# Retention attention and a gated layer on one core: 128-token units in the first block, another order of W_in slabs, other engines for their casts

## The chip, the cores and the metric

The kernel runs on one core of a Trainium2 chip. A core has TensorE (PE) for matrix products, VectorE (DVE), ScalarE (ACT), GpSimd (POOL) and SyncE (SP), which here only issues transfers. PE reads its operands from the on-chip memory SBUF and writes into PSUM, eight banks of 2 KB per partition. Every engine works through its own written list of instructions in order; semaphores hold it where it needs what another engine or a transfer makes. The metric is the device time of one execution in microseconds (us).

## What is computed

```python
def _attn_ref(q, k, v):                      # batch 8, heads 8, 576 positions, 64 wide
    scores = scale * np.matmul(q, k.transpose(0, 1, 3, 2))
    gamma = 1.0 - 2.0 ** (-5.0 - np.arange(H))
    Dmat = np.where(rel >= 0, gamma[:, None, None] ** rel[None, :, :], 0.0)
    return np.matmul(scores * Dmat[None], v)

x = attn_out.transpose(0, 2, 1, 3).reshape(4608, 512)
h = x @ w_in                                 # 512 x 2048
g = h * np.cos(h)
return g @ w_out                             # 2048 x 512
```

Inputs and output are float32; the kernel works in bf16 on PE.

## The kernel before, in words

**Attention.** The decay is folded into V and Q, so a causal product of plain masks is left: each batch row is cut into chunks of 64 positions, and a running state (K transposed times V) carries the past. The chunks are worked in 37 *sessions*; the first eight are "big" ones, handled in pairs (0/1, 2/3, 4/5, 6/7). For a pair, SP loads K, Q and V (`load_kv` L433, `load_q` L452, 512 KB each). K is cast to bf16 (`cast_k`, L494 on DVE or POOL, L491 on ACT), Q and V are cast and scaled (`cast_q` L532, `cast_v` L515). PE transposes K and Q (`step_tk` L552, `step_tq` L565), and a copy brings the result to SBUF (`turn`, L541 on DVE, L540 on ACT). Then come the scores (`big_s`: PE L704, DVE mask L712, four masks a pair), the state (L738), its copy to `sbd` (`ev_st`, DVE L667), the products with V (L763) and with the state (L730), and the eviction into `xt`, the layer's input (`move`, ACT L680). Later sessions take smaller steps (L608, L617, L627, L638, mask L653), and their loads are smaller (L441, V cast L522). Late sessions do not use PE for the transposes but a DMA transpose issued by SP (`move_k` L574, `move_q` L580): `BYPE` in `schedule` is the first session for which this holds.

**The layer.** Tokens are worked in nine blocks of 512. `mlp1` is one *unit* of the first layer, one PSUM bank: four matmuls (depth 512) for each 128 columns of W_in, either one such group over 512 tokens or several over fewer (PE L844); ACT makes the cosine (L852), DVE multiplies (L855) into `gt`. Block 0's second layer is a plain product (`mlp2`, L869). Blocks 1 to 8 use seven half-size products in place of eight (`strassen`, `product`, L963), for which DVE and POOL first make sums of `gt` (`token_sums`: L923, L928, L932) and DVE sums of W_out (`weight_sums`: L902, L908); the results are put together at L998, L1002 and L1007.

**Weights.** W_in comes in eight slabs of 256 columns (`load_win` L466, 512 KB each, f32), which land in tensors that are needed only later (`gt`, `s5`, `tw`: `staged`), and are cast into `win` (`cast_win`, L494 or L491). Slab s serves column groups 2s and 2s+1. W_out comes by four casting transfers from POOL (`load_wout` L483), held until a K load has landed.

**What sets the order.** `schedule` adds operations in a chosen sequence, `Prog.arrange` then plays them through a list scheduler with costs, a window for each engine and PSUM banks (`Box`), and writes the final order of every engine; until a planned time (`FILL`) it puts filler matmuls (`fill`, L828) where PE has nothing else. Constants steer it:

- `WP[s]`: the item of the load list ahead of which slab s is loaded. `WC[s]`: the engine that casts slab s.
- `EQ`, `C1`: engines for the casts of Q (two halves), for the first quads and for those after.
- `UNITS`: first-layer units of block 0 as (first token, last token, column groups). A unit takes 512 / (number of tokens) groups. `EARLY`: how many of them are added ahead of the attention of the next sessions.
- `G1`, `G2`: how many sessions' loads are listed at the start.
- `HOLD`: how many half products of `strassen` are kept back to the end of a block (the second number is for the last block but one).
- `POOLED`: from which block on the sum L928 runs on POOL instead of DVE.

The line of `schedule` that names the engines for the first four sessions is L1157, with the copy of K's transposes at L1159.

Of the kernel before, what the change touches and what calls it, by code (L numbers as in the profile page):

```python
# [18 lines left out]
TB = 512  # L19
NTB = TOK // TB  # L20
NB = 6
HOLD = (1, 4)
LS = (0, 1, 4, 2, 3, 5)
AT = (9, 11, 13, 15)
C1 = ('pool', ('pool', 'pool'), 'pool')
EO, ES, EQ = ('act', 'act'), ('dve', 'act'), ('dve', 'pool')
WP = (6, 5, 7, 8, 6, 9, 10, 9)
WC = ("pool", "act", "act", "pool", "pool", "act", "act", "dve")
G1, G2, WG = 3, 4, ("stg", 1, 1, 0)
EARLY = 2  # L30
SOFT = ()
SG = (1, 3)
UNITS = ((0, 256, (0, 10)), (256, 512, (0, 10)), (0, 512, (10, 16)))
FILL, SLOW = 24.0, 5.6
NF = DFF // 128
HF, HB = NF // 2, TB // 2
# [204 lines left out]


SOLO = 8
POOLED = 4
STB = 0


# [46 lines left out]
def new_in(g, of):  # L294
    was = {of(*x)[0] for y in SES[:g] for x in y}
    return [x for x in dict.fromkeys(of(*x)[0] for x in SES[g]) if x not in was]
# [6 lines left out]
class Kernel:  # L303
# [610 lines left out]
    def token_sums(self, j, u):  # L914
# [5 lines left out]
        def keys(k, *ts):  # L920
            return [("gt", j % 2, f + HF * k + i, x) for i in range(2) for t in ts for x in range(4 * t, 4 * t + 4)]
# [4 lines left out]
            r=keys(0, 0, 1) + keys(1, 0, 1), w=[("s5", f), ("s5", f + 1)], cost=0.62, port=True, lazy=True)  # L926
        eng = "pool" if j >= POOLED else "dve"
        self.P.add(eng, lambda e: e.tensor_tensor(  # L928
# [139 lines left out]
    def schedule(self):  # L1068
# [2 lines left out]

        need = [req(TB * (j + 1)) for j in range(NTB)]
        tiles, quads = ([new_in(g, of) for g in range(NS)] for of in (tile_of, quad_of))
        BYPE, LEAD = 14, 2
        at = {"load": 0, "cast": 0}

        def load_to(g, gate=()):
            while at["load"] < min(g, NS):
                x = at["load"]
                ts = [t for t in tiles[x] if t >= SOLO or t % 2 == 0]  # L1080
                for t in ts:
                    self.load_kv(t, 0, gate)
                for k in quads[x]:
                    self.load_q(k, gate)
                for t in ts:
                    self.load_kv(t, 1, gate)
                at["load"] += 1

        def cast_to(g, k="pool", q=("pool", "pool"), v="pool"):
            while at["cast"] < min(g, NS):  # L1090
                x = at["cast"]
                assert x < at["load"]
                for t in self.twos(tiles[x]):
                    self.cast_k(t, k)
                for y in quads[x]:
                    self.cast_q(y, q)
                for t in tiles[x]:
                    self.cast_v(t, v)
                at["cast"] += 1

        def T(g):
            if g >= NS:
                return
            if g < BYPE:
                for k in quads[g]:
                    self.step_tq(k, "dve")
                for t in self.twos(tiles[g]):
                    self.step_tk(t, "dve")
            x = g + LEAD
            if BYPE <= x < NS:  # L1110
                for k in quads[x]:
                    self.move_q(k)
                for t in tiles[x]:
                    self.move_k(t)
            cast_to(min(g + LEAD + 2, need[1]), *C1)
            cast_to(g + LEAD + 2)
            load_to(g + LEAD + 4)

        def run(mlp, att):
            n, m, k = len(att), len(mlp), 0  # L1120
            for i, u in enumerate(mlp):
                u()
                while k < n * (i + 1) // m:
                    att[k]()
                    k += 1

        def att_of(g0, g1):
            out = []
            for g in range(g0, g1):
                if BIG[g] or BIG[g - 1]:  # L1130
                    out.append(lambda g=g: self.step_s(g))
                out += [lambda g=g: T(g + 1), lambda g=g: self.step(g, not BIG[min(g + 1, NS - 1)]), lambda g=g: self.ev_st(g)]
            return out

        def m1(lo, hi, *fs):
            return lambda: self.mlp1(lo, hi, fs)
# [8 lines left out]
        def begin(lo, hi):  # L1145
            for i in range(lo, hi):
                for s in range(8):
                    if min(WP[s], len(items) - 1) == i and s not in SOFT and s - 1 not in SOFT:
                        self.load_win(s)
# [4 lines left out]
        for x, t in zip(SOFT, SG):  # L1154
            self.load_soft(x, [("stg", t, 0, 0)])
        for g in range(need[0]):
            cast_to(g + 1, "act", EQ, "dve" if g == 3 else "pool")  # L1157
            for t in self.twos(tiles[g]):
                self.step_tk(t, "dve")  # L1159
            for k in quads[g]:  # L1160
                self.step_tq(k, "dve")
            self.step_s(g)
            self.step(g, False, EO)
            self.ev_st(g, ES)
        begin(n0, len(items))
        for x in range(8):
            if x not in SOFT and x - 1 not in SOFT:
                self.cast_win(x, WC[x])
        for x in range(4):
            self.load_wout(x, [WG])  # L1170
        load_to(G2 + need[0], [("wout", 0)])
        cast_to(need[0] + 2, *C1)
        units = [(lo, hi, range(f, f + 512 // (hi - lo))) for lo, hi, fs in UNITS for f in range(*fs, 512 // (hi - lo))]
        for lo, hi, fs in units[:EARLY]:
            self.mlp1(lo, hi, fs)
        run([m1(lo, hi, *fs) for lo, hi, fs in units[EARLY:]], [lambda: T(need[0])] + att_of(need[0], need[0] + 2))
        sums = [x for y in zip(self.weight_sums(0), self.weight_sums(1)) for x in y]
# [6 lines left out]
        for j in range(1, NTB):  # L1184
# [3 lines left out]
            for f in range(0 if last else NF):  # L1188
                if j > 1:
                    mlp.append(m1(TB * (j + 1), TB * (j + 2), f))  # L1190
                elif f % 2 == 0:
                    mlp.append(m1(1280, 1536, f, f + 1))
                mlp += two[f:min(f + 1, 14 - HOLD[j + 2 == NTB])]
                if f in AT:
                    mlp.append(lambda u=AT.index(f), j=j: self.token_sums(j + 1, u))
            mlp += two[14 - HOLD[j + 2 == NTB]:14 if not last else 0]
            run(mlp, att_of(need[j + 1], need[j + 2]) if j + 2 < NTB else [])
# [38 lines left out]
```

## Time and profile before

| | us |
|---|---|
| median of 4 runs | 299.72 (299.58 to 300.63) |
| the profiled execution | 299.58 |
| its span | 297.8 |
| PE busy | 288.7 (97%) |
| DVE busy | 232.1 (78%) |
| ACT busy | 186.8 (63%) |
| POOL busy | 173.3 (58%) |

The granted TensorE clock is full (1.0). PE's busy time includes the filler, and the ends of pipelined matmuls are modelled, so a busy PE is not one at its peak. The averages hide stages: the first 20 us are set by loads, later ones by other things. In the rows of the profile, `bk` is a PSUM bank, `st` the state in PSUM, `stg` and `qstg` the f32 landing buffers of K, V and Q, `nat` and `qnat` their bf16 copies, `kt` and `qt` the transposed ones, `pt` the masked scores. A row gives its start, its length, engine, line, operation, output and input, the count, and in brackets the idle time ahead of it and what ended that.

### The profile page before, as it was taken

What the parts mean: (1) busy time and instruction counts of PE and PEld (TensorE: products, weight loads), DVE (VectorE), ACT (ScalarE), POOL (GpSimd) and SP (SyncE); (2) the same over time, 40 slices, a digit from 0 to 9 for tenths busy, and PEclk for the clock granted to TensorE, in tenths of its full rate; (3) what the DMA queues carried; (4) which work ended last, traced back from release to release, by engine and by line L of the source; (5) the groups of instructions that cost most, each with busy time, mean ns of one, the idle gap of its engine ahead of it and who ended that gap; (6) DMA issues with size and microseconds to landing.
All of it is one profiled execution on the core that took longest, in us unless ns stands there. A gap on an engine that the chain in (4) does not pass through costs nothing.

```text
span 297.8 us, 8942 instructions
## 1 busy us (share of the span) xinstructions
PE 288.7 (97%) x3751; PEld 203.7 (68%) x3751; DVE 232.1 (78%) x369; ACT 186.8 (63%) x317; POOL 173.3 (58%) x166
## 2 busy tenths in 40 slices
PE   6988899999999999999999999999999999999996
PEld 2557468765788885767566766676677577666685
DVE  6775899999789389679957995898489739964951
ACT  6256767836598286676667667766776777555521
POOL 4566650878847587287508992899274017402923
PEclk9999999999999999999999999999999999999999
DMA  7999999998999999989789988988201011102024
GB/s 207 303 327 325 279 192 218 207 220 207 201 247 209 192 277 203 220 170 200 166 183 234 203 175 212 212 149 191 59 33 60 16 44 40 45 19 70 2 70 143
DMA packets 123896, 50.13 MB, mean 168 GB/s; under 512 B 82384, under 2 KB 123344, under 8 KB 123856
## 3 DMA queue, kind: packets, MB, share of 16 engines
q1 hardware_dynamic: 121744, 47.46, 70.7%
q0 software_dynamic: 2112, 2.10, 4.3%
q8 instruction: 30, 0.49, 0.8%
q14 instruction: 10, 0.08, 0.1%
HBM read 36.70 MB, written 9.44 MB: 155 GB/s over the span
## 4 chain that ended last, share of the span: by engine, by line
PE 87%; SPq 4%; DMA 3%; DVE 3%; ACT 2%; issue 1%; DVEq 0%
PE bk L844 39%; PE bk L963 33%; PE bk L869 5%; DMA gt<-in_moe_w_in_dram 3%; PE st L638 2%; PE bk L617 2%; SPq L433 2%; SPq L466 1%; PE bk L608 1%; DVE gt L855 1%; PE bk L627 1%; PE bk L565 1%; SPq L452 1%; PE bk L552 1%; ACT xt L680 1%; DVE pt L712 1%
## 5 line engine op out<-in xcount | busy, mean ns | idle before, releaser
L844 PE MATMUL bk<-xt,win 128*128 128x512 bf16 (+1 forms) x744 | 138.9, 331 | 2.8 <-ACT win L491 0.7
L852 ACT ACTIVATE cb<-bk,cpi 128x512 bf16<-128x512 f32 x144 | 98.4, 688 | 55.2 <-PE bk L844 51.5
L855 DVE TENSOR_TENSOR gt<-bk,cb 128x512 bf16<-128x512 f32 x144 | 96.3, 684 | 41.8 <-ACT cb L852 36.5
L844 PEld LDWEIGHTS bk<-xt,win 128*128 128x128 bf16 x744 | 70.8, 98 | 43.7 <-issue 1.0
L532 POOL TENSOR_TENSOR qnat<-qstg,wt 128x512 bf16<-128x512 f32 x34 | 40.1, 1198 | 20.8 <-DMA qstg<-in_q_dram 19.0
L998 POOL TENSOR_TENSOR sv<-sv,os 128x512 f32<-128x512 f32 x16 | 20.4, 1273 | 49.1 <-ACT os L1007 36.3
L680 ACT ACTIVATE sbd<-st 64x512 bf16<-64x512 f32 x58 | 34.3, 592 | 11.7 <-PE bk L608 10.2
L494 POOL CAST nat<-stg 128x512 bf16<-128x512 f32 x32 | 24.7, 778 | 20.4 <-DMA stg<-in_k_dram 15.8
L928 POOL TENSOR_TENSOR s<-gt 128x512 bf16<-128x512 bf16 x20 | 28.8, 1448 | 13.4 <-DVE gt L855 13.4
L932 DVE TENSOR_TENSOR gt<-gt 128x1024 bf16<-128x1024 bf16 x32 | 34.1, 1067 | 0.2
L522 POOL TENSOR_TENSOR nat<-stg,wt 128x512 bf16<-128x512 f32 x28 | 32.1, 1147 | 2.4 <-DMA stg<-in_v_dram 1.9
L963 PE MATMUL bk<-tw,gt 128*128 128x256 bf16 x256 | 32.1, 273 | 0.0
L963 PE MATMUL bk<-wout,s 128*128 128x256 bf16 x256 | 31.6, 273 | 0.2 <-DVE s L923 0.2
L923 DVE TENSOR_TENSOR s<-gt 128x1024 bf16<-128x1024 bf16 x32 | 29.0, 916 | 3.1 <-PE bk L963 2.8
L963 PE MATMUL bk<-wout,gt 128*128 128x256 bf16 x256 | 30.8, 273 | 0.0
L680 ACT ACTIVATE xt<-bk 128x256 bf16<-128x256 f32 (+1 forms) x64 | 26.9, 488 | 4.2 <-DVE pt L653 3.6
L963 PEld LDWEIGHTS bk<-wout,s 128*128 128x128 bf16 x256 | 24.5, 98 | 6.5 <-DVE s L923 0.7
L963 PEld LDWEIGHTS bk<-tw,gt 128*128 128x128 bf16 x256 | 24.2, 98 | 6.0 <-ACT sv L1002 0.6
L963 PEld LDWEIGHTS bk<-wout,gt 128*128 128x128 bf16 x256 | 24.8, 98 | 4.4
L653 DVE TENSOR_TENSOR pt<-bk,tri 128x256 bf16<-128x256 f32 (+3 forms) x39 | 20.4, 543 | 0.8 <-PE bk L608 0.4
L1007 ACT ACTIVATE os<-bk 128x512 f32<-128x512 f32 x16 | 9.6, 597 | 12.0 <-PE bk L963 11.9
L998 POOL TENSOR_TENSOR sv<-sv 128x512 f32<-128x512 f32 x8 | 12.9, 1610 | 6.6 <-ACT sv L1002 6.3
(76 smaller groups left out, 276.6 us busy)
## 6 DMA issues: line engine op xcount, KB each, us to landing
out_dram<-os SPq DMA_DIRECT2D x31, 256.0 KB, 3.4
qstg<-in_q_dram SPq DMA_DIRECT2D x12, 512.0 KB, 5.8
stg<-in_k_dram SPq DMA_DIRECT2D x24, 256.0 KB, 4.5
stg<-in_v_dram SPq DMA_DIRECT2D x24, 256.0 KB, 5.1
stg<-in_k_dram SPq DMA_DIRECT2D x4, 512.0 KB, 7.6
stg<-in_v_dram SPq DMA_DIRECT2D x4, 512.0 KB, 7.4
gt<-in_moe_w_in_dram SPq DMA_DIRECT2D x4, 512.0 KB, 8.5
wout<-in_moe_w_out_dram POOLq DMA_DIRECT2D x4, 512.0 KB, 12.7
```

Of the source, the lines that this page charges most:

```text
L494: self.P.add(eng, lambda e: e.tensor_copy(dst, src), r=r, w=w, cost=cost, port=eng == "pool" or half == 0.75)
L522: self.P.add(eng, lambda e: e.tensor_tensor(ap(self.NAT[na], 2 * DM, 0, 128, DM, [D, H], [1, D]), ap(self.STG[st], 2 * DM, 0, 128, DM, [D, ...
L532: self.P.add(eng, lambda e, x=x: e.tensor_tensor(ap(self.QNAT[slot], 2 * DM, 0, 128, x * DM, [D, H], [1, D]), ap(self.QSTG[slot], 2 * DM, ...
L680: self.P.add(eng, (lambda e: e.activation(*io(), AF.Copy)) if eng == "act" else (lambda e: e.tensor_copy(*io())), r=r, w=w, cost=0.175 + 0 ...
L844: inst = e.matmul(self.bk(box.i, 0, 128, i * n, n), ap(self.WIN, 4 * DFF, 0, 128, c * DFF + 128 * f, [1, 128]), ap(self.XT, 4 * XR, 0, 128 ...
L852: self.P.add("act", lambda e: e.activation(ap(cb, TB, 0, 128, 0, [1, m]), self.bk(box.i, 0, 128, 0, m), AF.Sin, bias=self.CPI.ap(), scale= ...
L855: self.P.add("dve", lambda e: e.tensor_tensor(ap(gt, NF * TB, 0, 128, f0 * TB + lo - TB * j, [TB, len(fs)], [1, n]), self.half_bank(box.i, ...
L923: self.P.add("dve", lambda e: e.tensor_tensor(ap(self.S5, HF * TB, 0, 128, f * TB, [1, 2 * TB]), ap(gt, NF * TB, 0, 128, f * TB, [1, 2 * TB]),
L928: self.P.add(eng, lambda e: e.tensor_tensor(ap(self.S1, HF * HB, 0, 128, f * HB, [HB, 2], [1, HB]), half(0, 0), half(1, 1), ALU.add), r=ke ...
L932: self.P.add("dve", lambda e: e.tensor_tensor(ap(gt, NF * TB, 0, 128, f * TB + HB, [HF * TB - HB, 2], [TB, 2], [1, HB]), ap(gt, NF * TB, 0 ...
L963: inst = e.matmul(self.bk(box.i, 0, 128, at * HB, HB), ap(lt, lsize, 0, 128, loff + f * lstep + 128 * t, [1, 128]), ap(rt, rsize, 0, 128, ...
L998: self.P.add(eng, lambda e: e.tensor_tensor(out(), a(), b(), op), r=r, w=w, cost=1.2 if eng == "pool" else 0.09 + 0.00104 * n * HB, port=e ...
```

## The change

It sets other values for the constants, and other engines in two calls:

```diff
-HOLD = (1, 4)
+HOLD = (2, 4)
-C1 = ('pool', ('pool', 'pool'), 'pool')
-EO, ES, EQ = ('act', 'act'), ('dve', 'act'), ('dve', 'pool')
-WP = (6, 5, 7, 8, 6, 9, 10, 9)
-WC = ("pool", "act", "act", "pool", "pool", "act", "act", "dve")
-G1, G2, WG = 3, 4, ("stg", 1, 1, 0)
-EARLY = 2
+C1 = ('pool', ('dve', 'pool'), 'pool')
+EO, ES, EQ = ('act', 'act'), ('dve', 'act'), ('pool', 'dve')
+WP = (5, 6, 7, 6, 9, 8, 9, 7)
+WC = ("pool", "dve", "dve", "pool", "dve", "pool", "act", "act")
+G1, G2, WG = 5, 5, ("stg", 1, 1, 0)
+EARLY = 4
-UNITS = ((0, 256, (0, 10)), (256, 512, (0, 10)), (0, 512, (10, 16)))
+UNITS = ((0, 128, (0, 4)), (0, 256, (4, 8)), (128, 256, (0, 4)), (256, 512, (0, 8)), (0, 512, (8, 16)))
-POOLED = 4
+POOLED = 5
-        BYPE, LEAD = 14, 2
+        BYPE, LEAD = 15, 2
-            cast_to(g + 1, "act", EQ, "dve" if g == 3 else "pool")
+            cast_to(g + 1, "pool", EQ, "dve" if g < 2 else "pool")
             for t in self.twos(tiles[g]):
-                self.step_tk(t, "dve")
+                self.step_tk(t, "act")
```

- Block 0's first layer: the first 256 tokens of column groups 0 to 3 are worked as two units of 128 tokens by four groups; groups 4 to 7 keep 256-token units; groups 8 to 15 (before: 10 to 15) take all 512 tokens at once. The number of units stays 16.
- W_in slabs are loaded in the order 0, 1, 3, 2, 7, 5, 4, 6 (before: 1, 0, 4, 2, 3, 5, 7, 6). Slabs 1, 2 and 4 are cast on DVE, 0, 3 and 5 on POOL, 6 and 7 on ACT.
- In the first sessions K is cast on POOL (before: ACT), the first V load on DVE (before: POOL), the halves of Q change places between DVE and POOL, and K's transposes are copied by ACT (before: DVE). For the next two quads of Q, DVE casts one half (before: POOL both).
- Of the transposes that SP issues as DMA transposes, that of session 14's K goes to TensorE.
- Two half products are held back at the end of most blocks (before: one), and the sum L928 of block 4 runs on DVE (before: POOL).

Since the scheduler plays all this through, instructions also change places on the other engines.

## The prediction

> **What bounds the kernel now.** I read the slices first, then the stretches, then the order of time of the first 60 us.
>
> ```profile
> PE   6988899999999999999999999999999999999996
> DVE  6775899999789389679957995898489739964951
> DMA  7999999998999999989789988988201011102024
> ```
>
> PE is full from the fourth slice on; the DMA engines are full for the first 28 slices. What PE does in the first slices is partly filler (L828). So I counted the useful matmuls in PE's order (filler left out) at the spacing each kind shows in an undisturbed run: 109 ns for 256 columns (1.75 us for 16 at L844), 216 ns for 512 (2.59 for 12), 56 ns for a transpose (0.45 for 8). They sum to 272.5 us. The span is 297.8, so 25.3 us are lost: clock less useful work done is 19.2 us at 46.1, 20.0 at 78.9, 21.5 at 150.0 and 22.5 at 274.1; the tail is the rest. The start, where the change works, holds most of it.
>
> ```profile
> 16.30:24.40 8.10, 6.66 (x140) 4.75 (x141) 6.01 (x11) 4.44 (x6) 4.51 (x6) 1.00 1.14 324
> 24.40:46.20 21.80, 19.79 (x281) 13.87 (x282) 17.49 (x30) 14.57 (x22) 13.42 (x15) 1.00 1.16 256
> 46.20:79.00 32.80, 32.80 (x466) 22.97 (x466) 30.59 (x49) 20.66 (x37) 24.02 (x23) 1.00 0.98 208
> ```
>
> Columns: stretch, length, then busy time of PE, PEld, DVE, ACT, POOL, the granted clock, DMA, GB/s. From 24.4 to 46.2 DVE has 4.3 us of idle time; from 46.2 to 79 it is busy 93% while PE is full: the two are level there. A gain at the start must be a gain on both.
>
> ```profile
> 13.69 1.06 ACT L491 ACTIVATE win<-gt 128x1024 bf16<-128x1024 f32 x1 [2.17 <-DMA gt<-in_moe_w_in_dram]
> 17.74 2.48 DVE L712 TENSOR_TENSOR pt<-bk,trb 128x512 bf16<-128x512 f32 x4 [1.38 <-PE bk L704]
> 18.34 1.04 POOL L494 CAST win<-gt 128x1024 bf16<-128x1024 f32 x1 [0.79 <-DMA gt<-in_moe_w_in_dram]
> 24.23 1.31 ACT L680 ACTIVATE xt<-bk 128x512 bf16<-128x512 f32 x2
> 24.38 1.05 PE L844 MATMUL bk<-xt,win 128*128 128x256 bf16 x8 [0.70 <-ACT win L491]
> 31.87 0.68 DVE L494 CAST win<-tw 128x1024 bf16<-128x1024 f32 x1
> 33.27 3.19 POOL L483 DMA_DIRECT2D wout<-in_moe_w_out_dram  x4 [2.88 <-DMA stg<-in_k_dram]
> 53.95 0.75 DVE L902 TENSOR_TENSOR tw<-wout 128x1024 bf16<-128x1024 bf16 x1
> ```
>
> The first slab of W_in lands at 13.7 and is cast on ACT; the next lands at 18.3; ACT evicts tokens 256 to 511 only at 24.23, since a slab cast (L491, 23.27) stands ahead of it; PE waits 0.70 us for that cast. Those are the places that the change touches.
>
> **The change, part by part.** The order of instructions of both builds gives what moves.
>
> *SP's queue.* The 20 loads at its head are full-size (512 KB), and issue plus time to landing puts the slots at 4.9, 6.7, 8.5, 10.3, 12.1, 13.7, 15.4, 18.3, 19.8, 21.6, 23.3, 24.9, 26.5, 28.3, 29.8, 31.3, 33.0, 34.6, 36.3, 37.7 us. Only what stands in a slot changes: slab 0 at 13.7, slab 1 at 18.3, slab 3 at 19.8, slab 2 at 23.3, slab 7 at 24.9, Q of sessions 4/5 at 26.5 (was 24.9), slab 5 at 28.3, V at 29.8 (was 28.3), slab 4 at 31.3, slab 6 at 33.0, K of sessions 6/7 at 34.6 (was 33.0); Q and V after it stay. G1 and G2 move no load in the order.
>
> *First layer of block 0.* The first unit now needs slabs 0 and 1 (4 columns of 128 tokens) instead of slab 1 alone. Slab 1 is cast on DVE: 18.35 to 19.05 by the 0.68 us of L494 above. So PE's first L844 starts at 19.1 instead of 16.3; slab 3 on POOL (1.04) gives the second unit at 20.9. Behind slab 1's cast on DVE stand the four masks L712 of sessions 2/3, ready at about 17.2: they run 19.05 to 21.5 instead of 17.74 to 20.2, 1.3 us late. Then sbd (L667), the state on PE (22.2), L763 and L730 (23.4). ACT, which has no cast there any more, evicts at 23.1 to 24.5 instead of 25.54. At 24.75 PE stands where it stood at 23.5 with the same units done, but before it then waited for slab 2 (to 24.38); now slab 2 is cast on DVE by 24.1. From there five 256-column units run without a wait (24.75 to 29.1), Q's transposes, two 512 units to 31.3. The next masks (L704 to 32.0, DVE to 34.5) hold four banks, so PE waits about 1 us (32.3 to 33.3), then five units, to 37.6. W_out's issue (L483) waits for K at 34.6 and ends at 37.85, the K cast behind it on POOL at 39.05, and PE's transposes of it follow at 39.6. At 44.4 PE has done what before it had done at 46.1: 1.8 us ahead.
>
> DVE is not: it gets two V casts, two Q halves and two slab casts more (6 x 0.68), and gives up two copies to ACT. From 18.35 to the end of the masks of sessions 4/5 it has 37 instructions to the last unit's product, 22.6 us at the 0.61 us of a step in its rows of several (1.87 for 3, 2.48 for 4), then 6 more, with about 1 us of waits: 45.7 us, against 46.2 before. So the lead is 0.5 us on DVE and 1.8 on PE. Since both are nearly full to 79 us, I take 1.0, nearer DVE's. **-1.0** (from +1.5, if DVE idles 2 us more than I find, to -1.8).
>
> *Width.* 32 matmuls of 128 columns, 8 more of 512, 32 fewer of 256: the trace has no 128-column L844. The nearest row is a full-array matmul of 128 columns with its own weight load, L565: 56 ns. 32 x 0.056 + 8 x 0.216 - 32 x 0.109 = +0.04 us. The Trainium skill speaks against this ("TensorE: Matmul & The Clock Gate", section Back-to-back issue gap): a sustained stream of weight load and 128-column matmul is said to take about 81 ns each, which would make it +0.8 us. The same line gives 131 ns for 512 columns, where this trace has 216, so I keep the row.
>
> *Engines of the casts.* K's first two casts move from ACT to POOL (0.59 us each in its row of two, as on ACT), the copies of their transposes from DVE (0.68) to ACT (1.05, by L491 of the same 1,024 columns), the first V casts from POOL to DVE ahead of Q's copy: the masks of sessions 0/1 start at 11.2 instead of 10.83, hidden because slab 1 ends only at 19.05. "SBUF — State Buffer", section Who interferes with whom: a DVE instruction with two SBUF inputs blocks a GpSimd one that reads SBUF[...]. The row agrees once: L532 on POOL took 1.55 beside DVE's L532 (6.88) and 1.04 alone. By the row, each two-input cast moved to DVE can cost POOL 0.5, at most 4 x 0.5 = 2.0 us; but from 10 to 31 us POOL waits for loads before nearly every cast, which covers it. Without that cover slab 3 comes 0.5 late, and the second unit with it. **0** (to +0.5).
>
> *BYPE.* One session's K (session 14, four transposes) moves from SP to PE and a copy of 0.41 us to DVE: 4 x 0.056 = **+0.2**; SP loses one DMA transpose (1.2 to 1.3 us of issue), on a path where nothing waits. PE is full there, so the 0.2 is paid.
>
> *HOLD and POOLED.* At two block ends PE waits: 0.36 us at 118.5 and 0.21 at 148.2 (for DVE's L923 and what hangs behind it). Holding a second half product puts 8 x 0.109 = 0.87 us of cover there: 0 to -0.6, **-0.2** taken, since other units move too. POOLED puts four sums of 0.67 us on DVE in a block where DVE is busy 73%: 0; if one stands ahead of an L923 at that end, +0.7.
>
> Sum: -1.0 + 0.04 + 0.2 - 0.2 = -1.0 us on the profiled run's 299.58 (span 297.8 and 1.8 around it) makes 298.6; that run is 0.14 below the median of the four, so **298.7** against 299.7. 0.3% (0.9 us) is about what a measurement can tell from no change, so this is just faster.
>
> **Rivals.** *The gain is taken back at W_out* (same, 299.5). The last W_out load lands at 52.8 (35.7 + 17.1) and L902 reads it at 53.95. In the new order L902 comes after as many products (24) as before, and W_out is issued 1.4 us later. If all of that reaches the landing, 54.2, DVE's lead there is gone, at a point where it is nearly full: start 0.0, rest 0.0 to -0.3. For it: the DMA engines are full until 52. Against: loads sharing them would come earlier instead, and W_out then ends nearly as before.
>
> *DVE becomes the bound* (slower, 301.2). One mechanism: DVE is first in, first out in its written order, and slab casts that wait for a DMA (slab 1, 18.3; slab 2, 23.3; slab 4, 31.3; Q's halves) now stand ahead of masks and products. Before, ACT and POOL stood in those waits. The masks already lose 1.3 us at 17.74. It decides from the point where the masks of sessions 4/5 end after 46.2 us, that is, once DVE idles over 1.5 us between 24 and 46 us; it idled 4.3 there before. At 3 us of idle they end at 47.7: +1.5, with nothing later to win it back before 79.
>
> **How the numbers follow.** My case 0.44, W_out's 0.25, DVE's 0.31. The likeliest one's own range is 297.6 to 299.2 (start -1.8 to -0.5). The range reaches to DVE's case at 301.3, where under 1 in 10 is left above, and to 297.6 below. Faster 0.43, same 0.26, slower 0.31.
>
> **What would show it.** First L844 at 19.1, not 16.3; masks of sessions 2/3 at 19.05; tokens 256 to 511 evicted by 24.5; masks of sessions 4/5 ended by 45.7; useful work at 79 us 1 us ahead; L902 without a wait. I am wrong if DVE shows waits for slab DMAs over 3 us in all (1.9 of it ahead of slab 1), or if 128-column matmuls stand 80 ns apart.

## The result, and the profile after

| | us | ratio to before, 95% interval |
|---|---|---|
| before | 299.72 (298.87 to 301.74) | |
| changed kernel | 299.41 (297.83 to 303.02) | 0.9989 [0.9978, 1.0000] |
| changed kernel, measured again beside the experiments | 299.82 (297.95 to 302.28), before 299.71 | 1.0012 [0.9995, 1.0029] |

The change makes no difference that can be measured. The forecast of 298.7 was 0.7 to 1.1 us too low, inside its range of 297.6 to 301.3. The execution of 303.02 ran in a slower state, at a granted clock of 0.994, and is in no ratio. The other runs of the changed kernel still spread more widely than those of before (standard deviation 0.86 against 0.59 us), and its profiled execution took 298.1 us (span 296.3), 1.3 below its own median. What the profile after shows of the start is found again in the other executions; that it keeps its gain to the end is not.

One stretch of the profile after (length, busy time of PE, PEld, DVE, ACT and POOL, granted clock, DMA, GB/s):

```profile
24.40:46.20 21.80, 20.42 (x287) 14.33 (x286) 20.98 (x35) 14.44 (x22) 12.53 (x14) 1.00 1.15 257
```

From 24.4 to 46.2 DVE goes from 17.49 to 20.98 us busy: its 4.3 us of idle time are down to 0.8, the clock is still full, and the DMA engines move what they moved before. The same stretch in order of time, lines that answer to those shown of before:

```profile
18.02 0.69 DVE L494 CAST win<-gt 128x1024 bf16<-128x1024 f32 x1 [1.34 <-DMA gt<-in_moe_w_in_dram]
18.62 2.47 DVE L712 TENSOR_TENSOR pt<-bk,trb 128x512 bf16<-128x512 f32 x4
...
19.96 1.94 PE L844 MATMUL bk<-xt,win 128*128 128x128 bf16 x24 [1.13 <-DVE pt L712]
22.89 1.06 PE L844 MATMUL bk<-xt,win 128*128 128x128 bf16 x16
...
22.77 1.35 ACT L680 ACTIVATE xt<-bk 128x512 bf16<-128x512 f32 x2
...
34.57 3.19 POOL L483 DMA_DIRECT2D wout<-in_moe_w_out_dram  x4 [3.20 <-DMA stg<-in_k_dram]
...
42.99 2.47 DVE L712 TENSOR_TENSOR pt<-bk,trb 128x512 bf16<-128x512 f32 x4
...
50.79 1.29 DVE L902 TENSOR_TENSOR tw<-wout 128x1024 bf16<-128x1024 bf16 x2 [0.74 <-DMA wout<-in_moe_w_out_dram]
...
54.15 0.69 DVE L902 TENSOR_TENSOR tw<-wout 128x1024 bf16<-128x1024 bf16 x1 [0.33 <-DMA wout<-in_moe_w_out_dram]
```

Slab 1's cast on DVE waits 1.34 us for its load, the masks L712 follow it, and PE's first L844 waits 1.13 us for a PSUM bank that the masks give free. ACT has evicted tokens 256 to 511 by 24.12 (L680). The 128-column matmuls take 1.06 us for 16, their tail included. The masks of sessions 4/5 end at 45.46 (before: 46.2), and at 44.56 PE has done the useful work that before it had done at 46.13.

### The profile page after: what moved, and what is told of

Same layout as the page of the kernel before. It is cut to its first block, busy times and chain, and to the rows that moved or that the text cites. A ratio compares the mean times of both kernels' runs of the same rounds, so it can differ in the third digit from the quotient of the medians.

```text
span 296.3 us, 8973 instructions
## 1 busy us (share of the span) xinstructions
PE 288.4 (97%) x3763; PEld 203.7 (69%) x3763; DVE 234.2 (79%) x377; ACT 185.0 (62%) x313; POOL 166.2 (56%) x162
## 4 chain that ended last, share of the span: by engine, by line
PE 81%; DVE 6%; DMA 6%; SPq 4%; issue 1%; ACT 1%; POOL 0%
PE bk L844 35%; PE bk L963 33%; PE bk L869 5%; DMA stg<-in_k_dram 3%; DMA s<-in_moe_w_in_dram 3%; DVE gt L855 2%; PE st L638 2%; PE bk L617 2%; SPq L466 1%; SPq L433 1%; PE bk L608 1%; PE bk L627 1%; DVE pt L712 1%; SPq L452 1%; PE bk L565 1%
## 5 line engine op out<-in xcount | busy, mean ns | idle before, releaser
L844 PE MATMUL bk<-xt,win 128*128 128x512 bf16 (+2 forms) x752 | 137.7, 329 | 2.4 <-DVE pt L712 2.4
L855 DVE TENSOR_TENSOR gt<-bk,cb 128x512 bf16<-128x512 f32 x144 | 95.5, 683 | 37.0 <-ACT cb L852 35.9
L844 PEld LDWEIGHTS bk<-xt,win 128*128 128x128 bf16 x752 | 70.6, 98 | 42.9 <-DVE pt L712 3.2
L532 POOL TENSOR_TENSOR qnat<-qstg,wt 128x512 bf16<-128x512 f32 x32 | 36.9, 1171 | 18.8 <-DMA qstg<-in_q_dram 18.8
L680 ACT ACTIVATE sbd<-st 64x512 bf16<-64x512 f32 x58 | 34.3, 592 | 13.1 <-PE bk L608 11.8
L494 POOL CAST nat<-stg 128x512 bf16<-128x512 f32 x36 | 25.9, 726 | 27.6 <-DMA stg<-in_k_dram 27.6
L522 POOL TENSOR_TENSOR nat<-stg,wt 128x512 bf16<-128x512 f32 x28 | 33.9, 1212 | 5.5 <-DMA stg<-in_v_dram 5.4
L963 PE MATMUL bk<-wout,gt 128*128 128x256 bf16 x256 | 31.6, 273 | 0.0
L923 DVE TENSOR_TENSOR s<-gt 128x1024 bf16<-128x1024 bf16 x32 | 29.0, 912 | 3.0 <-PE bk L963 2.8
L963 PE MATMUL bk<-tw,gt 128*128 128x256 bf16 x256 | 31.3, 273 | 0.0
L932 DVE TENSOR_TENSOR gt<-gt 128x1024 bf16<-128x1024 bf16 x32 | 30.8, 964 | 0.2
L680 ACT ACTIVATE xt<-bk 128x256 bf16<-128x256 f32 (+1 forms) x64 | 26.8, 489 | 6.2 <-DVE pt L653 4.8
L928 POOL TENSOR_TENSOR s<-gt 128x512 bf16<-128x512 bf16 x16 | 23.0, 1443 | 10.4 <-DVE gt L855 10.3
L653 DVE TENSOR_TENSOR pt<-bk,tri 128x512 bf16<-128x512 f32 (+3 forms) x38 | 20.3, 551 | 0.2 <-PE bk L608 0.2
L1002 ACT ACTIVATE sv<-bk 128x512 f32<-128x512 f32 x16 | 9.6, 597 | 14.9 <-PE bk L963 14.8
```

The source lines that it names most:

```text
L494: self.P.add(eng, lambda e: e.tensor_copy(dst, src), r=r, w=w, cost=cost, port=eng == "pool" or half == 0.75)
L522: self.P.add(eng, lambda e: e.tensor_tensor(ap(self.NAT[na], 2 * DM, 0, 128, DM, [D, H], [1, D]), ap(self.STG[st], 2 * DM, 0, 128, DM, [D, ...
L532: self.P.add(eng, lambda e, x=x: e.tensor_tensor(ap(self.QNAT[slot], 2 * DM, 0, 128, x * DM, [D, H], [1, D]), ap(self.QSTG[slot], 2 * DM, ...
L680: self.P.add(eng, (lambda e: e.activation(*io(), AF.Copy)) if eng == "act" else (lambda e: e.tensor_copy(*io())), r=r, w=w, cost=0.175 + 0 ...
L844: inst = e.matmul(self.bk(box.i, 0, 128, i * n, n), ap(self.WIN, 4 * DFF, 0, 128, c * DFF + 128 * f, [1, 128]), ap(self.XT, 4 * XR, 0, 128 ...
L855: self.P.add("dve", lambda e: e.tensor_tensor(ap(gt, NF * TB, 0, 128, f0 * TB + lo - TB * j, [TB, len(fs)], [1, n]), self.half_bank(box.i, ...
```

## The experiments

In what follows *loss* is the clock less the useful matmuls done so far, in TensorE's own order and at the spacings of the prediction, read where a session's L617 starts. *The start* means every edit of the change but HOLD, POOLED and BYPE. Up to 82 us the start alone, the whole change and the start with any of the three give TensorE the same list.

### Which half of the change does what

The start alone:

```diff
-HOLD = (2, 4)
+HOLD = (1, 4)
-POOLED = 5
+POOLED = 4
-        BYPE, LEAD = 15, 2
+        BYPE, LEAD = 14, 2
```

> The changed kernel with HOLD, POOLED and BYPE set back: the new start alone. Its first 80 us are instruction for instruction those of the changed kernel. If the start is worth what the prediction summed (-1.0 us), the median is 298.7. If W_out takes the start's gain back in most runs, it is 299.4 to 299.7. If the rest of the change costs time and hides a gain of the start, it is faster than the changed kernel, 298.9 or less against 299.4.

> The start alone once more. If its 298.58 was a property of the kernel: 298.3 to 298.9, ratio under 0.998. If its first 6 runs were a lucky sample (the changed kernel's own runs go from 297.8 to 303, since VectorE's sums of 0.68 us take up to 1.5 us beside a GpSimd operation and loads decide which of them meet): about 299.2 with runs spread over 2 us.

Measured twice: 298.58 (ratio 0.9963 [0.9948, 0.9978], 6 runs) and 298.55 (0.9971 [0.9954, 0.9988], 22 runs). The start alone is 0.9 to 1.1 us faster than before (by the ratios, and by the medians) and has the lowest median in this study.

The other half, HOLD (2, 4), POOLED 5 and BYPE 15 on the start of before:

> The kernel before with HOLD, POOLED and BYPE of the change and nothing else. By the prediction's sum 0.0 us (+0.2 for the transposes, -0.2 for the cover at block ends): 299.7, and no wait of TensorE for a sum at the ends of blocks 1 and 2. If this part costs what the start gains, it is 300.2 to 300.7.

299.55, ratio 0.9991 [0.9977, 1.0005]: nothing. And the whole change once more:

> The changed kernel once more, for a second profile beside these. W_out theory: in an execution that takes 299.4 or more the waits of L902 are longer than 1.1 us in all. Slab theory: DVE waits longer for the transfers of slabs 1, 2 and 4 and of Q (1.3, 0 , 0 and 0.4 us in the first profile). If neither, the difference of runs lies after 80 us.

It gave the 299.82 of the table. In its profiled execution (299.78) L902 waits for W_out 0.33 us in all, less than in the profile after, and slab 1's cast waits 1.6 us, 0.3 more. So most of the 1.7 us between the two profiled executions arise after 82 us. The two halves do not add: by the medians, -1.1 and -0.15 make 298.4, and the whole is 1.0 to 1.4 us above that.

### W_out's landing

In `settle`, which works out who waits for whom, the DMA issues of POOL no longer wait for the K load; the order on every engine stays:

```diff
-            r = [("bk", k.i) if isinstance(k, Box) else k for k in op.r]
+            r = [("bk", k.i) if isinstance(k, Box) else k for k in (() if op.eng == "pool" and op.ring else op.r)]
```

> The changed kernel, same order on every engine, but the W_out transfers no longer wait for the K load (POOL issues them about 31.4 us instead of 34.6). W_out theory: the waits of L902 for W_out (0.74 and 0.33 us in the profile of the changed kernel) are gone, DVE keeps its lead, and the median falls by 0.7 to 1.0, to 298.5. If the lead is lost elsewhere, the median stays at 299.4; if the four transfers delay K of sessions 6/7 and what follows it, it rises to 300.

299.82, ratio 0.9997 [0.9985, 1.0009]. L483 starts at 31.70 instead of 34.57 us and both waits of L902 are gone, with no gain. W_out is not where the gain went.

### HOLD, POOLED and BYPE one by one

Each is added alone to the start.

> The new start with HOLD (2,4) alone; POOLED 4 and BYPE 14 stay. The start alone measured 298.58 (0.9963 of before), all of the change 299.4 and 299.8: one of HOLD, POOLED and BYPE, or their sum, gives about 1 us back. Prediction's step: HOLD wins 0 to 0.6 us at the block ends, so 298.0 to 298.6. Rival (HOLD is what gives the start back: the held products leave less for TensorE at other places): 299.3 or more, with TensorE's loss from 115 to 170 us up by 0.7 or more against the start alone (+1.4 there).

> The new start with POOLED 5 alone. Prediction's step: 0, up to +0.7 if a sum moved to VectorE stands ahead of an L923 at a block end: 298.6 to 299.3. Block 4 ends near 170 us, so a cost of this part must show after 155 us and nothing earlier. Rival (POOLED is what gives the start back): 299.3 or more, with the wait of L617 for L855 near 165 us (0.5 us in both profiles of the changed kernel, none with the start alone) there again.

> The new start with BYPE 15 alone: session 14's K transposed by TensorE. Prediction's step: +0.2 (four transposes of 56 ns), so 298.8. Rival (the copy of the transposes and the list that is planned anew around it cost more than TensorE's own time): 299.3 or more, with waits of TensorE between 90 and 125 us.

Times: HOLD 299.58 (0.9999 [0.9981, 1.0016]), POOLED 299.46 (0.9988 [0.9974, 1.0002]), BYPE 299.81 (1.0002 [0.9983, 1.0021]). Beside the start alone, which took 298.55 in the same sitting, these are 1.0, 0.9 and 1.3 us more (95% intervals from the single runs: 0.5 to 1.5, 0.5 to 1.3, 0.8 to 1.7). So each of the three takes back the start's gain by itself. The loss in the profiled executions, one for each row (us):

| | at 82 us | 82 to 107 | 107 to 170 | 170 to 200 | 200 to 255 |
|---|---|---|---|---|---|
| before | 20.0 | 0.1 | 1.5 | 0.2 | 0.5 |
| rest only | 20.0 | 0.1 | 1.1 | 0.2 | 0.6 |
| start alone | 19.3 | 0.1 | 1.2 | 0.3 | 0.5 |
| start alone, again | 18.6 | 0.2 | 1.4 | 0.3 | 0.5 |
| start and HOLD | 19.3 | 0.4 | 1.9 | 0.2 | 0.7 |
| start and POOLED | 19.2 | 0.1 | 1.4 | 1.1 | 0.4 |
| start and BYPE | 19.6 | 0.3 | 1.9 | 0.3 | 0.5 |
| start and BYPE, one cast held back (next section) | 18.8 | 1.0 | 0.7 | 0.3 | 0.5 |
| whole change, profile after | 18.6 | 0.5 | 0.9 | 0.2 | 0.4 |
| whole change, again | 18.9 | 0.5 | 2.3 | 0.3 | 0.4 |

So the start's gain is there in every row that has the start, though by 0.4 to 1.4 us, and what differs between the versions is how much is lost at the block ends from 107 to 200 us.

The two rows of the whole change are one program: 0.9 and 2.3 us. Most of the difference falls in two places, 0.8 us from 114 to 130 us (end of block 1) and 0.5 from 135 to 145 (end of block 2). The profile after:

```profile
113.79 0.68 DVE L932 TENSOR_TENSOR gt<-gt 128x1024 bf16<-128x1024 bf16 x1
...
115.65 0.67 DVE L923 TENSOR_TENSOR s<-gt 128x1024 bf16<-128x1024 bf16 x1
...
138.56 0.41 DVE L928 TENSOR_TENSOR s<-gt 128x512 bf16<-128x512 bf16 x1
138.90 0.68 DVE L932 TENSOR_TENSOR gt<-gt 128x1024 bf16<-128x1024 bf16 x1
139.50 0.68 DVE L923 TENSOR_TENSOR s<-gt 128x1024 bf16<-128x1024 bf16 x1
...
140.13 2.29 POOL L532 TENSOR_TENSOR qnat<-qstg,wt 128x512 bf16<-128x512 f32 x2 [1.44 <-DMA qstg<-in_q_dram]
```

And the same instructions in the second execution:

```profile
114.31 1.52 DVE L932 TENSOR_TENSOR gt<-gt 128x1024 bf16<-128x1024 bf16 x1
...
117.02 1.43 DVE L923 TENSOR_TENSOR s<-gt 128x1024 bf16<-128x1024 bf16 x1
...
139.59 0.92 DVE L928 TENSOR_TENSOR s<-gt 128x512 bf16<-128x512 bf16 x1
140.43 1.53 DVE L932 TENSOR_TENSOR gt<-gt 128x1024 bf16<-128x1024 bf16 x1
141.88 1.53 DVE L923 TENSOR_TENSOR s<-gt 128x1024 bf16<-128x1024 bf16 x1
...
139.19 2.23 POOL L532 TENSOR_TENSOR qnat<-qstg,wt 128x512 bf16<-128x512 f32 x2 [2.02 <-DMA qstg<-in_q_dram]
...
144.45 0.39 PE L617 MATMUL bk<-qt,sbd 128*128 128x64 bf16 x8 [0.29 <-issue]
```

POOL's cast of Q starts when its load lands. At the end of block 2 the three sums of DVE take 0.41, 0.68 and 0.68 us where the cast comes after them. Where it comes 0.4 us ahead of them, they take 0.92, 1.53 and 1.53, 2.2 us more in all, and PE, which waits for nothing there in the profile after, now does. The same kernel gets one or the other by when a load lands.

For HOLD and POOLED the rows say something else: there the new list of operations matters, and long sums alone do not cost. The end of block 2 with the start alone, then with HOLD:

```profile
140.46 1.53 DVE L923 TENSOR_TENSOR s<-gt 128x1024 bf16<-128x1024 bf16 x1
...
141.91 1.26 DVE L928 TENSOR_TENSOR s<-gt 128x512 bf16<-128x512 bf16 x1
```

```profile
140.94 1.53 DVE L923 TENSOR_TENSOR s<-gt 128x1024 bf16<-128x1024 bf16 x1
...
142.38 1.26 DVE L928 TENSOR_TENSOR s<-gt 128x512 bf16<-128x512 bf16 x1
...
144.95 0.39 PE L617 MATMUL bk<-qt,sbd 128*128 128x64 bf16 x8 [0.76 <-issue]
```

These two sums are equally long. From 137 to 146 us the start alone loses nothing in this execution and 0.4 us in the other one; with HOLD it is 0.9. (From 114 to 130 us HOLD's cover works as it was meant to: 0.2 us of loss, against 0.8 and 1.0 with the start alone. From 130 to 137 us it loses another 0.6, where L617 waits for a product behind an L923 of 1.33 us: there the length of a sum has its part.) Block 4 with the start alone, then with POOLED:

```profile
172.52 0.69 DVE L855 TENSOR_TENSOR gt<-bk,cb 128x512 bf16<-128x512 f32 x1 [0.41 <-ACT cb L852]
...
173.13 1.01 DVE L932 TENSOR_TENSOR gt<-gt 128x1024 bf16<-128x1024 bf16 x1
```

```profile
172.93 1.00 DVE L932 TENSOR_TENSOR gt<-gt 128x1024 bf16<-128x1024 bf16 x1
173.85 1.27 DVE L855 TENSOR_TENSOR gt<-bk,cb 128x512 bf16<-128x512 f32 x2
...
174.63 0.39 PE L617 MATMUL bk<-qt,sbd 128*128 128x64 bf16 x8 [0.18 <-issue]
```

L932 is equally long in both, but with POOLED the products stand behind it, and L617 starts 0.1 us after the first of them ends. Another 0.5 us is lost up to 183 us, where the three sums take 0.68, 0.42 and 1.10 us.

### One cast held back

To test whether a long sum is a cause, the start with BYPE was run with the same order on every engine and one wait more: POOL's cast of a Q (the 79th operation of its list) waits for DVE's L932 (the 173rd).

```diff
-        self.settle()
+        self.settle(), hold(self, 78, 172)
...
+def hold(prog, late, first):
+    op = [x for x in prog.ops if x.eng == "pool"][late]
+    by = [x for x in prog.ops if x.eng == "dve"][first]
+    op.deps.append(by)
```

> The start with BYPE 15, the order of every engine as it was (299.81), but GpSimd's cast of one Q (L532, at 112.3 us) waits until VectorE's sum L932 ahead of the product L855 is done; in that execution L928 took 1.06 and L932 1.52 us beside the cast, and TensorE's L617 waited 1.23 us for the L855 behind them. Theory (the sums are lengthened by GpSimd's operation, and that is what TensorE waits for): L928 about 0.4 and L932 0.68 us there, the wait of L617 under 0.3, TensorE's loss at 118 us 1.0 to 1.5 us lower; 298.5 to 299.0 if nothing later takes it back. Rival (the new plan has the product behind the sums, GpSimd has no part in it): wait still 0.8 or more, 299.8.

The start with BYPE, without the wait:

```profile
113.71 1.06 DVE L928 TENSOR_TENSOR s<-gt 128x512 bf16<-128x512 bf16 x1
114.70 1.52 DVE L932 TENSOR_TENSOR gt<-gt 128x1024 bf16<-128x1024 bf16 x1
116.14 0.68 DVE L855 TENSOR_TENSOR gt<-bk,cb 128x512 bf16<-128x512 f32 x1
...
112.29 2.21 POOL L532 TENSOR_TENSOR qnat<-qstg,wt 128x512 bf16<-128x512 f32 x2 [0.85 <-DMA qstg<-in_q_dram]
...
116.88 0.41 PE L617 MATMUL bk<-qt,sbd 128*128 128x64 bf16 x8 [1.23 <-DVE gt L855]
```

With it:

```profile
113.65 0.42 DVE L928 TENSOR_TENSOR s<-gt 128x512 bf16<-128x512 bf16 x1
113.98 0.68 DVE L932 TENSOR_TENSOR gt<-gt 128x1024 bf16<-128x1024 bf16 x1
114.70 0.69 DVE L855 TENSOR_TENSOR gt<-bk,cb 128x512 bf16<-128x512 f32 x1
...
114.75 2.49 POOL L532 TENSOR_TENSOR qnat<-qstg,wt 128x512 bf16<-128x512 f32 x2 [3.21 <-DVE gt L932]
...
115.44 0.41 PE L617 MATMUL bk<-qt,sbd 128*128 128x64 bf16 x8
```

The two sums take 0.42 and 0.68 us, the product L855 starts 1.44 us sooner, PE's wait of 1.23 us is gone, and the time falls from 299.81 to 298.85 (ratio 0.9972 [0.9954, 0.9989]). The two medians come from different sittings (before: 299.64 and 299.51) and the second from 9 runs; their difference is 0.96 us, with a 95% interval of 0.5 to 1.4. The two profiled executions alone would not show it so well: the held one happens to be 0.8 us ahead at 82 us and loses 0.7 more from 82 to 107 us, ahead of the held cast, with a wait of 0.68 us at 94.89 that has no releaser in the profile. Only the 1.2 us less from 107 to 170 us can be the cast's.

For BYPE the cause is shown: not the 0.2 us of its transposes, but a cast on POOL that overlaps two sums in the new plan. The plan has its part in it: with the start alone the product L855 (113.12) stands ahead of L928, and there L928 took 1.04 us beside a cast at no cost. For HOLD and POOLED no such run was made. That their sums stand behind a cast is seen; how much of their loss is the new list and how much the length of the sums stays open.

### GpSimd's casts with one input

```diff
-        self.P.add(eng, lambda e: e.tensor_tensor(
+        self.P.add(eng, lambda e: e.tensor_scalar(
             ap(self.NAT[na], 2 * DM, 0, 128, DM, [D, H], [1, D]),
-            ap(self.STG[st], 2 * DM, 0, 128, DM, [D, H], [1, D]),
-            ap(self.WT, NW, 0, 128, 8 * (TILES[t][1] % NR), [1, H], [0, D]), ALU.mult),
+            ap(self.STG[st], 2 * DM, 0, 128, DM, [D, H], [1, D]), 1e-6, None, ALU.mult),
```

The same is done in `cast_q` for the sessions from the ninth on, where its lambda then stands on L533. This kernel leaves out the scaling by position.

> All of the change, same order on every engine, but GpSimd's casts of Q and V for the sessions from the ninth on take one input (times a constant) instead of two: the scaling by position is left out, the work of all engines else is the same. Theory (VectorE's sums L923, L932 and L928 are lengthened by GpSimd's two-input casts, and the changed kernel's time hangs on which of them meet): the casts fall from 1.04 to some 0.6 us, the sums' mean from 0.90 to 1.02 to under 0.85, TensorE's loss from 100 to 170 us falls from 1.3 to 2.6 to under 1.0, and the time to 298.0 to 298.6. Rival (the plan's own order makes TensorE wait): sums shorter, time still 299.3 to 299.9.

299.42, ratio 1.0001 [0.9991, 1.0011]. The groups of this kernel from 82 to 290 us (count, busy time, mean ns, idle time ahead), then those of the whole change in its second execution:

```profile
L522 POOL TENSOR_SCALAR nat<-stg 128x512 bf16<-128x512 f32 x22 | 34.0, 1545 | 4.0 <-DMA stg<-in_v_dram 2.4
...
L932 DVE TENSOR_TENSOR gt<-gt 128x1024 bf16<-128x1024 bf16 x29 | 25.9, 895 | 0.2
L923 DVE TENSOR_TENSOR s<-gt 128x1024 bf16<-128x1024 bf16 x29 | 24.1, 840 | 3.0 <-PE bk L963 2.8
```

```profile
L932 DVE TENSOR_TENSOR gt<-gt 128x1024 bf16<-128x1024 bf16 x29 | 29.6, 1024 | 0.2
L923 DVE TENSOR_TENSOR s<-gt 128x1024 bf16<-128x1024 bf16 x29 | 27.6, 959 | 3.0 <-PE bk L963 2.8
L522 POOL TENSOR_TENSOR nat<-stg,wt 128x512 bf16<-128x512 f32 x20 | 23.8, 1191 | 5.4 <-DMA stg<-in_v_dram 3.4 <-PE bk L608 2.0
```

One expectation missed outright: the one-input form takes POOL 1.55 us on average, not 0.6, longer than the two-input form. TensorE then waits 1.6 us for a cast of Q before 79 us, and the loss at 82 us is 21.4. The others hold in the main in spite of that: the two groups of sums fall by 7.2 us in all though POOL is busy longer (their mean to 0.87 us, where under 0.85 was expected), and from 107 to 170 us TensorE loses 0.4 us, against 0.9 and 2.3. From 82 us on it loses 1.1 us, the least of all kernels here. The time answers to neither theory, since the start lost what the block ends gained.

### Three casts held back in the whole change

```diff
-        self.settle()
+        self.settle(), hold(self, 78, 173), hold(self, 93, 204), hold(self, 104, 230)
```

> All of the change with the same order on every engine, but three casts of Q on GpSimd (L532, at 114.7, 140.1 and 161.4 us in the profile after) wait until VectorE has made the sums at the end of the block (L932 at 113.8, L923 at 139.5 and L923 at 163.1 us). If the lengthened sums are what makes the changed kernel give the start's gain back: L932 and L923 at the end of blocks 1 and 2 take 0.68 us, not 1.53; TensorE's loss from 100 to 170 us, 1.3 in the profile after and 2.6 in its second one, falls to 1.0 or less, and the time to 298.3 to 298.9 with a narrower spread. Rival (the delayed casts are late for the transposes, or the lengthening moves to the next sums): the loss stays at 1.3 or more, and 299.3 to 299.9.

299.39, ratio 0.9988 [0.9971, 1.0006]: no gain that can be measured. At the three places it does what it should: from 107 to 170 us the loss is 0.4 us. Then, at the end of block 3:

```profile
168.24 2.49 POOL L532 TENSOR_TENSOR qnat<-qstg,wt 128x512 bf16<-128x512 f32 x2
...
168.67 1.15 DVE L932 TENSOR_TENSOR gt<-gt 128x1024 bf16<-128x1024 bf16 x1
169.75 1.53 DVE L923 TENSOR_TENSOR s<-gt 128x1024 bf16<-128x1024 bf16 x1
171.20 1.26 DVE L928 TENSOR_TENSOR s<-gt 128x512 bf16<-128x512 bf16 x1
...
174.17 0.39 PE L617 MATMUL bk<-qt,sbd 128*128 128x64 bf16 x8 [0.99 <-issue]
```

The third held cast ends at 166.54, and POOL's next operations, V, K and the following Q, run behind it without a wait straight into the next sums: 1.4 us are lost from 170 to 200. A cast that is moved out of one sum's way can stand in the next one's, and this experiment's rival was right. So no run shows that the whole change would keep the start's gain if its sums stayed short.

### The start with the units of before

```diff
-UNITS = ((0, 128, (0, 4)), (0, 256, (4, 8)), (128, 256, (0, 4)), (256, 512, (0, 8)), (0, 512, (8, 16)))
+UNITS = ((0, 256, (0, 10)), (256, 512, (0, 10)), (0, 512, (10, 16)))
```

> The start alone, with the first-layer units of before in it (256 tokens by column groups 0 to 9, then 10 to 15): order of slabs, engines of casts and EARLY as in the start. It tells whether the 128-token units carry the start's gain. Prediction's step: the units' width is worth +0.04 by itself, the gain comes from casts that VectorE and GpSimd make before TensorE needs them, so most of the 1.0 us at 79 us should stay (loss at 79 us 18.6 to 19.3). Rival (the narrow units are what fills TensorE's wait for slabs and banks between 16 and 46 us): loss at 79 us near 20.0, as before.

299.63, ratio 1.0003 [0.9986, 1.0020], loss at 82 us 19.9. The gain of the start is gone, so the rival is nearer.

These units ask for slabs in the order 0 to 4, while the loads bring 0, 1, 3, 2, 7 first, so it is shown that the other slab order and cast engines alone do not carry the gain; whether the width of 128 tokens does, or only that units and slab order fit each other, stays open.

## Why the prediction was right or wrong

*Start, -1.0: right.* The loss at 82 us is 18.6 to 19.6 (mean 19.1) in the ten profiled executions that have the start's list unchanged, against 20.0 in both with the old one: 0.4 to 1.4 us, mean 0.95. (The kernel with one-input casts, which adds waits of its own there, is left out.) The ends of the estimate, 0.5 for DVE and 1.8 for PE, read in the profile after as 0.74 (masks of 4/5) and 1.6. The number was in part luck, since its working had errors that cancelled: the first L844 came at 19.96, not 19.1, since a bank was missing behind the late masks and not the slab; later units started earlier than reckoned (24.23, not 24.75). And with the units of before, the other slabs and casts give 0.1 us of the 1.0.

*Width, +0.04: right.* Sixteen 128-column L844 in 1.06 us with their tail are about 56 ns apart, so the trace's row stands, and not the 81 ns of the Trainium skill ("TensorE: Matmul & The Clock Gate", section Back-to-back issue gap).

*Engines of the casts, 0: right at the start.* POOL's L532 at 26.16 took 1.55 us beside DVE, as before, under cover of its wait for a load.

*BYPE +0.2, HOLD and POOLED -0.2: the step that failed.* Their sum of 0 holds on the old start (299.55). On the new one each alone costs 0.9 to 1.3 us. The prediction priced BYPE by its transposes, HOLD by the matmuls it holds as cover, and POOLED by whether DVE has room in a block that is 73% busy, with +0.7 as its worst case. It took a sum's length as fixed (0.67 us in POOLED's term). That number is already a mean: the twelve L928 on DVE in the profile before take 0.41 to 1.49 us, and its group of L932 has a mean of 1.07. The runs show 0.68 us for 1,024 columns where POOL is not beside the sum, up to 1.53 at the block ends otherwise. The Trainium skill ("SBUF — State Buffer", section Who interferes with whom) says that a DVE instruction with two SBUF inputs contends with a GpSimd one that reads SBUF, and that the order of issue decides which of them is held up; the counts in the last section agree. The prediction used it in one direction only, for what POOL loses at the start; what DVE loses to POOL at the block ends, where PE waits for DVE, was left out. That the new lists put other products behind the sums was left out too. One reading was wrong besides: the wait of 0.36 us at 118.5, put down to L923, ends in the trace with ACT's eviction, as the row says:

```profile
118.54 1.02 PE L844 MATMUL bk<-xt,win 128*128 128x512 bf16 x4 [0.36 <-ACT xt L680]
```

*The rivals.* W_out did show waits (0.74 and 0.33 us), but taking them away gains nothing. DVE as the bound through slab casts: 1.34 us of wait ahead of slab 1 and 0.8 us of idle time from 24 to 46 us are below the 1.5 at which it was to decide; the masks of 4/5 ended earlier than before. "Same" came true by a way that neither rival names. The forecast held by the width of its range: the likeliest case, faster, had 297.6 to 299.2 for itself, and both medians lie above that.

## What to carry to other kernels

An instruction's duration is not always a constant of its row: compare the shortest and the longest of a group, and look at what ran beside the long ones. A long instruction costs time only where something that TensorE waits for stands behind it, so look at the order too. A gain at the start reaches the end only if later stages keep it, and here they depend on how casts that start when a load lands fall against such sums; so parts of a change that are worth nothing alone can cost the gain of another. Judge such constants by several executions and by the loss at fixed points of the work, not by one profile.

## What the runs showed of the hardware

In the fourteen profiles, DVE's sums of two bf16 inputs, 1,024 columns, go two ways. The 263 that no POOL operation overlaps take 0.67 to 0.69 us. The others take up to 1.72, and which of the two began first decides: of 166 that began ahead of POOL's operation, none took over 0.72 us; of 528 that began while one still had over 0.1 us to run, 479 did. Sums of 512 columns go from 0.41 to 1.50 us in the same way.

Beside POOL's one-input multiplication or a plain cast alone, the sums reached 1.10 and 1.11 us at most. The one-input multiplication itself took 1.49 us in most cases and up to 2.04. That is slower than the two-input multiplication (1.04 us where it runs freely) and the plain cast (0.61 us) of as many columns.
